# Loading the softmax factors of four attention chunks earlier, and finishing the first chunk on VectorE

## The chip, the cores and the metric

The kernel runs on one core of one Trainium2 chip. Its time is the device time of one execution in microseconds. A core has five engines that run beside each other, each with an instruction queue of its own that is worked off in order: TensorE (PE in the profile; its weight loads are listed as PEld), VectorE (DVE), ScalarE (ACT), GpSimd (POOL) and SyncE (SP). SP, ACT and POOL also issue DMA transfers. An instruction that waits for a semaphore holds up all that stands behind it in its queue.

## The reference, cut to what matters

The input `x` has 2048 rows of 640. Two branches share it. Branch A is attention with 32 heads of 20 over four chunks of 512 rows, softmax within the chunk (where a query's index is below the key's, the logit is pushed down by 1e9), mixed per head with a read from a memory that is summed over the chunks before; its output is multiplied by `wo`. Branch B is a gated feed-forward of width 1728. A gate per row mixes the two.

```
for s in range(4):
    logits = qs @ ks.T * scale + mask
    a_dot  = softmax(logits) @ vs
    a_mem  = (phi(qs) @ M) / (phi(qs) @ z + 1e-6)
    outs.append(g_head * a_mem + (1 - g_head) * a_dot)
    M, z = M + phi(ks).T @ vs, z + phi(ks).sum()
a = concat(outs) @ wo
b = (silu(x @ w1) * (x @ w3)) @ w2
return sigmoid(x . gate_w) * a + (1 - sigmoid(x . gate_w)) * b
```

## The kernel before, in words

All values are 32-bit; most products are made from a high and a low part in three passes (`PASSES`), so that a block of 128 x 512 results takes 15 matmuls over five blocks of 128 inputs. The chunks are handled in pairs, A = (0, 1) and B = (2, 3). For a pair the kernel projects v, k and q, stores q and k to DRAM by heads, and runs feed-forward groups; attention runs beside it all the time.

The order of TensorE's queue is the program's order, written out by hand. It is made by two generators. `attention()` yields 40 slots for each group of four heads; in slot 5 of 40 it emits a large group of score matmuls (`s`, `t`) and the product with v (`o`), in slot 17 a smaller one. In between, `step` takes feed-forward and projection work from a list of jobs, one step at a time; a step of that work is mostly three matmuls and ends with a `yield` of its nominal duration. Each step of it also calls `stores()` (which counts down the stores put off by `store_later`) and `w_step()` (which loads and splits weights ahead of use: two raw buffers, six split ones). The other engines' queues are ordered by Tile's planner: it takes what its own estimates of durations and transfers say is ready, earlier program order first. `here(...)` pins an instruction behind the one traced just before it on its engine. `after(n, f)` calls `f` n slots later; in the tail, a slot is a step.

The softmax denominators are handled at the end. The product with v also sums the probabilities. `pv_quad` stores its result to DRAM (`od`). When a chunk's last heads are done, `o_sums` loads the sums; 22 slots after the last product with v, `o_scale` (L670) turns them into factors `rs` on VectorE and writes them to DRAM, spread over 20 rows a head, in four transfers on ACT's queue (`rd`, L675). `normalize(c)` (L698) then does, for each of five blocks `b` of 128 rows:

- load the factors of the block, `rb`, on ACT's queue (L707), into one of two buffers of the tag `spread`;
- multiply the block of `oall` by it on VectorE (L716);
- for chunks 1 to 3, transpose the memory's part on TensorE into a PSUM bank (L720) and add it on VectorE (L721);
- cast the sum to its high part on ACT (L722) and take the difference as its low part on VectorE (L723).

Loads 0 and 1 are issued in the first step of this generator, load b + 2 at the start of the step after block b. The generator is braided into feed-forward steps: `braid(a, b, every, skip)` takes one step of `b` after each `every` steps of `a`, the first `skip` steps left out. Then `rest` (L783) multiplies by `wo`.

The matmul results go to eight PSUM banks, handed out in rotation. A matmul that begins a bank waits until the engine that empties the bank's last content is through: VectorE for row maxima (L588) and for the copy of an attention result (L638), ACT for exponentials (L620).

`finish(c, fb, ps)` (L508) ends a block of a chunk's output: add the accumulator, multiply by the row gate `shares[c]` (VectorE for odd blocks, POOL for even ones), store on SP's queue; for chunks 0 and 1 the store is put off by two steps. Chunk 0's `finish` lies at the switch from pair A to pair B. The buffer of its accumulator is taken over by pair B's `V`, which POOL first fills with ones (L348); POOL then splits weights (L106) and issues the loads of the k weights (L162).

Of the kernel before, what the change touches and what calls it, by code (L numbers as in the profile page):

```python
# [17 lines left out]
P = 128  # L18
# [20 lines left out]
def gated_mix(ctx: ExitStack, tc: tile.TileContext, xT, wqk, wv, w13, w2, w2h, wo, beta, out):  # L39
# [223 lines left out]
    def store_later(dst, src, key=None, queue=nc.sync, n=4):  # L263
        late.append([n, dst, src, key, queue])
# [177 lines left out]
    def job_read(c):  # L442
        return 5.6, memory_read(c)
# [64 lines left out]
    def finish(c, fb, ps, end=False):  # L508
        dst = accs[c][:, fb]
        for n0 in ((0, 256) if end else (0,)):  # L510
            d, p, g = (t[:, n0:n0 + (256 if end else L)] for t in (dst, ps, shares[c]))
            nc.vector.tensor_add(d, p, d)
            (nc.vector if end or fb % 2 else nc.gpsimd).tensor_mul(d, d, g)
            if c < 2:
                store_later(out[c, fb], d, n=2)
            else:
                nc.sync.dma_start(out[c, fb, :, n0:n0 + d.shape[-1]], d)

    def ffn_down(cs, js, idx, last=()):
        first = js[0] == 0  # L520
# [149 lines left out]
    def o_scale(c):  # L670

        here(nc.vector.reciprocal(rs, rs))
        nc.vector.scalar_tensor_tensor(rs, rs, cR, er, op0=ALU.mult, op1=ALU.mult)
        for a in range(4):
            here(nc.scalar.dma_start(rd[c][:, :, a * P:(a + 1) * P], rs[a::4].unsqueeze(1).broadcast_to([H, DH, P])))  # L675
        turned.append(c)

    shares = {}

    def spread(name):  # L680
        return sp.tile([P, L], F32, tag="spread", name=name, bufs=2)

    def load_share(c):
        shares[c] = spread(f"sh{c}")
# [4 lines left out]
    def load_memory(c):  # L689

        assert ("g", c, 3) in stored
        gms[c] = big_tile(f"gm{c}", FR)[:, :KB * L].rearrange("p (b n) -> p b n", b=KB)
        for qb in range(4):
            here(nc.gpsimd.dma_start(gms[c].bitcast(F32)[:, :, qb * P:(qb + 1) * P],
                                     gd[c][:, qb].rearrange("p (b n) -> p b n", b=KB)))
            yield 1

    def normalize(c):  # L698

        rows = rd[c].rearrange("h e n -> (h e) n")  # L700
        rb = {}

        def load(b):
            if b < KB:
                assert c in turned
                rb[b] = spread(f"rb{c}_{b}")
                here(nc.scalar.dma_start(rb[b], rows[b * P:(b + 1) * P]))  # L707

        load(0)
        load(1)  # L710
        yield 1
        if not c:
            gms[c] = big_tile(f"oT{c}", FR)[:, :KB * L].rearrange("p (b n) -> p b n", b=KB)
        for b in range(KB):
            o, hi = rb[b], gms[c][:, b]
            nc.vector.tensor_mul(o, oall[c][:, b].bitcast(F32), o)  # L716
            if c:
                pt = bank_tile(f"gt{c}_{b}")
                for qb in range(4):
                    nc.tensor.transpose(pt[:, qb * P:(qb + 1) * P], hi[:, qb * P:(qb + 1) * P].bitcast(F32), ident)  # L720
                nc.vector.tensor_add(o, o, pt)  # L721
            nc.scalar.copy(hi, o)  # L722
            nc.vector.tensor_sub(oall[c][:, b], o, hi.bitcast(F32))  # L723
            yield 450 if c else 1
            load(b + 2)

    NJ = NSEG * H

# [81 lines left out]
    def job_up(cs, j):  # L810
        return (4 if j < NF else 2) * 3.5, ffn_up(cs, j, plan_up([j])[0])
# [6 lines left out]
    def job_down(cs, g, last=()):  # L818
        return 2.32 * sum(3 if j < NF else 2 for j in GROUPS[g]), ffn_down(cs, GROUPS[g], plan_down(GROUPS[g]), last)

    def jobs_up(cs, g):
        return [job_up(cs, j) for j in GROUPS[g]]
# [17 lines left out]
    def chain(jobs):  # L840
        return sum(c for c, _ in jobs), (y for _, g in jobs for y in g)

    def braid(a, b, every, skip=0, rest=True):

        def gen():
            n = 0
            for y in a[1]:
                yield y
                n += not isinstance(y, float)
                if n > skip and (n - skip) % every == 0:  # L850
                    z = next(b[1], None)
                    if z is not None:
                        yield z
            if rest:
                yield from b[1]
        return a[0] + b[0], gen()
# [23 lines left out]
    d = job_down(A, 2)  # L880
    u = [job_up(A, j) for j in GROUPS[3][:2]]
    o1, o2 = jobs_oproj(0)
    seg = [d, braid(chain(u), o1, 5), o2] + [job_up(A, j) for j in GROUPS[3][2:]] + [job_down(A, 3)]
    u0, u1 = jobs_up_by_chunk(A, 4)
    x2, x3 = split_x(2), split_x(3)
    seg += [(0, load_raw(2)), (0, load_raw(3))] + u0 + [braid(chain(u1), (0, x2), 4, 0, False)]
# [13 lines left out]
    segs.append((2 * H + LAG + 2, seg))  # L900
    up.append(job_up(B, 2))
    o1, o2 = jobs_oproj(1)
    seg = [braid(chain(up[1:]), o1, 4, 11), braid(o2, job_read(3), 3, 1), job_down(B, 0), braid(chain(jobs_up(B, 1)), (0, load_memory(2)), 5)]
    segs.append((3 * H + LAG + 1, seg))
    d = job_down(B, 1)
    u = [job_up(B, j) for j in GROUPS[2][:2]]
    o1, o2 = jobs_oproj(2)
    seg = [d, braid(chain(u), o1, 5), o2] + [job_up(B, j) for j in GROUPS[2][2:]]
    seg += [job_down(B, 2), braid(chain(jobs_up(B, 3)), (0, load_memory(3)), 5)]
    segs.append((NJ + LAG, seg))  # L910
    d, u = job_down(B, 3), jobs_up(B, 4)
    o1, o2 = jobs_oproj(3)
    tail = [braid(chain([d] + u), o1, 5, 10)] + [o2, job_down(B, 4, B)]

    for n, (_, g) in enumerate(head):
        for _ in g:
# [112 lines left out]
```

## Time and profile before

| | us |
|---|---|
| median of 3 runs (lowest to highest) | 1131.23 (1129.55 to 1133.21) |
| the profiled execution, its own time | 1131.51 |
| its span, first to last instruction | 1129.7 |
| TensorE busy | 1099.9 |
| VectorE busy | 584.8 |
| POOL busy | 494.5 |
| ACT busy | 460.0 |
| mean granted TensorE clock | 0.989 |

The span is one execution; its own time is 1.8 us longer, for what lies around it. A row of the timeline reads: start in us, duration, engine, line, operation, what is written and read, how many merged, and in brackets the idle time of the engine before it with what ended it. A row of a stretch (a:b) reads: its length, the busy time of PE, PEld, DVE, ACT and POOL with instruction counts, the granted TensorE clock as a share of full speed, the busy share of the DMA engines, and GB/s. A row of the waits reads: who waited for whom, in total, how often, the longest. `rd` are the written factors, `rb` a loaded block of them, `gt` the transposed memory part, `oq` the copy of an attention result, `sh` the row gate.

### The profile page before, as it was taken

The page shows a single profiled execution, that of the slowest core. Times are in us where ns is not written, and L with a number is a line of the kernel's source. Part 1 is how long each engine was busy: PE and PEld are TensorE (multiplying, and loading weights), DVE is VectorE, ACT ScalarE, POOL GpSimd, SP SyncE. Part 2 cuts the span into 40 slices and gives each one's busy share as a digit, 9 for nine tenths or more (in the row PEclk, how much of TensorE's full clock was granted, in tenths as well). Part 3 has the DMA queues.
Part 4 walks back from the last instruction along what each step waited for, and adds up shares of the span by engine and source line. Part 5 has one row for each costly group of instructions (what it writes and reads, how often), then busy time and mean ns, then how long its engine had stood idle before and what let it go on. Part 6 is the DMA issues. An engine that isn't in the chain of part 4 may idle for free.

```text
span 1129.7 us, 17927 instructions
## 1 busy us (share of the span) xinstructions
PE 1099.9 (97%) x6265; PEld 856.5 (76%) x6265; DVE 584.8 (52%) x1689; ACT 460.0 (41%) x952; POOL 494.5 (44%) x601
## 2 busy tenths in 40 slices
PE   9999999999999999997999998999999989999998
PEld 6988877777777787785977776676777767777786
DVE  5032564455555455473253675774557665561465
ACT  6165334444243324254255543425544443334140
POOL 4053444354454346353153436444754544454232
PEclk9999999999999999998999999999999999999999
DMA  8265943344354345444286869355655533543323
GB/s 310 97 227 205 268 113 92 89 102 112 84 135 119 107 101 157 127 120 121 98 256 216 290 187 252 106 149 140 169 134 151 142 94 90 118 107 87 112 86 112
DMA packets 99193, 163.29 MB, mean 145 GB/s; under 512 B 10432, under 2 KB 34272, under 8 KB 99104
## 3 DMA queue, kind: packets, MB, share of 16 engines
q1 hardware_dynamic: 61312, 105.91, 29.9%
q0 software_dynamic: 20384, 38.68, 15.6%
q10 hardware_dynamic: 17408, 17.57, 4.9%
q8 instruction: 50, 0.82, 0.3%
q14 instruction: 39, 0.32, 0.1%
HBM read 101.80 MB, written 59.79 MB: 143 GB/s over the span
## 4 chain that ended last, share of the span: by engine, by line
PE 83%; DMA 4%; issue 4%; DVE 3%; POOL 3%; ACT 2%; SPq 0%; ACTq 0%; DVEq 0%; POOLq 0%
PE g L251 16%; PE f L534 15%; PE u L251 15%; PE k L251 6%; PE v L362 6%; PE q L251 6%; PE o L634 5%; PE s L581 4%; PE op L792 4%; PE t L614 3%; DMA rb<-rd 2%; PE pm L425 1%; PE nd L329 1%; POOL W L106 1%; ACT P L620 1%
## 5 line engine op out<-in xcount | busy, mean ns | idle before, releaser
L106 POOL TENSOR_TENSOR W<-wr,W 128x640 fp32r<-128x640 f32 (+1 forms) x126 | 197.0, 1570 | 280.1 <-ACT W L105 255.9
L588 DVE CUSTOM_DVE_ANT_0 junk<-s,mask 128x256 bf16<-128x256 f32 (+3 forms) x512 | 250.0, 488 | 115.3 <-PE s L581 82.9
L620 ACT ACTIVATE P<-t 128x512 f32<-128x512 f32 (+1 forms) x384 | 172.0, 538 | 132.5 <-PE t L614 104.3
L251 PE MATMUL g<-X,W 128*128 128x512 f32 x840 | 211.4, 400 | 2.5 <-DVE m L588 1.4
L251 PE MATMUL u<-X,W 128*128 128x512 f32 x780 | 197.4, 401 | 0.4 <-DVE m L588 0.4
L534 PE MATMUL f<-ht,W 128*128 128x512 f32 x820 | 195.2, 396 | 0.0
L251 PEld LDWEIGHTS g<-X,W 128*128 128x128 f32 x840 | 156.7, 189 | 40.1 <-DVE m L588 2.1
L534 PEld LDWEIGHTS f<-ht,W 128*128 128x128 f32 x820 | 153.1, 188 | 36.7
L624 POOL TENSOR_SCALAR_AFFINE_SELECT P<-P 128x256 f32<-128x256 f32 x192 | 93.4, 497 | 180.7 <-ACT P L620 180.4
L251 PEld LDWEIGHTS u<-X,W 128*128 128x128 f32 x780 | 145.2, 189 | 35.4 <-DVE m L588 0.6
L105 ACT CAST W<-wr 128x640 fp32r<-128x640 f32 (+1 forms) x133 | 95.6, 729 | 152.4 <-DVE acc L542 37.1
L106 POOL TENSOR_TENSOR ht<-ft,ht 128x512 fp32r<-128x512 f32 x52 | 67.8, 1304 | 112.2 <-ACT ht L105 112.2
L558 POOL DMA_DIRECT2D qk<-qkd x128 | 82.9, 649 | 2.3 <-PE t L614 1.2
L581 PE MATMUL s<-qk 60*128 60x256 f32 (+3 forms) x512 | 77.8, 346 | 2.8 <-DVE fu L491 1.0
L634 PE MATMUL o<-P,vg 128*32 128x512 f32 (+3 forms) x1024 | 77.7, 445 | 0.4 <-DVE X L131 0.4
L251 PE MATMUL k<-X,W 128*128 128x512 f32 x300 | 77.0, 403 | 0.7 <-ACT P L620 0.7
L251 PE MATMUL q<-X,W 128*128 128x512 f32 x300 | 75.3, 405 | 1.2 <-ACT X L105 0.4
L614 PE MATMUL t<-qk 62*128 62x256 f32 (+3 forms) x512 | 65.0, 324 | 9.8 <-DVE X L131 5.7
L362 PE MATMUL v<-W,X 128*128 128x320 f32 (+1 forms) x480 | 71.8, 311 | 0.0
L362 PEld LDWEIGHTS v<-W,X 128*128 128x128 f32 x480 | 71.1, 189 | 0.5 <-ACT P L620 0.2
L542 DVE TENSOR_TENSOR acc<-f,acc 128x512 f32<-128x512 f32 x65 | 44.4, 689 | 49.0 <-PE f L534 48.9
L251 PEld LDWEIGHTS q<-X,W 128*128 128x128 f32 x300 | 56.3, 191 | 17.0 <-ACT X L105 1.3
(107 smaller groups left out, 1084.1 us busy)
## 6 DMA issues: line engine op xcount, KB each, us to landing
qk<-qkd POOLq DMA_DIRECT2D x128, 240.0 KB, 4.4
wr<-in_w_dram SPq DMA_DIRECT2D x80, 320.0 KB
qkd<-qs SPq DMA_DIRECT2D x20, 512.0 KB
qkd<-ks SPq DMA_DIRECT2D x20, 512.0 KB
od<-oq SPq DMA_DIRECT2D x32, 256.0 KB
wr<-in_wo_dram SPq DMA_DIRECT2D x20, 320.0 KB
vg<-vd SPq DMA_DIRECT2D x16, 336.0 KB
xr<-in_xT_dram SPq DMA_DIRECT2D x20, 256.0 KB
```

Of the source, the lines that this page charges most:

```text
L105: pin(nc.scalar.copy(dst[:, 0], src))
L106: (lo or nc.gpsimd.tensor_sub)(dst[:, 1], src, dst[:, 0].bitcast(F32))
L251: nc.tensor.matmul(ps, w[:, a, kb * P:(kb + 1) * P], x[:, b, kb, :], start=n == 0, stop=n == 14)
L362: nc.tensor.matmul(ps[:, :n1 - n0], x[:, a, kb, lb * P:(lb + 1) * P], wvt[kb][:, b, n0:n1], start=n == 0, stop=n == 14)
L534: nc.tensor.matmul(ps, w, h, start=n == 0, stop=n == len(ms) - 1)
L558: here(nc.gpsimd.dma_start(t[64 * i:64 * i + RH], qkd[c][RH * (h + i):RH * (h + i + 1)]))
L581: nc.tensor.matmul(ps[i][:, o:o + w], q[:, qb * P:(qb + 1) * P], key[:, :w], start=n == 0, stop=n == len(todo) - 1, skip_group_check=True)
L588: nc.vector.tensor_tensor_reduce(out=junk[:, :w], in0=ps[i][:, o:o + w], in1=mask[:, L - w:], scale=1.0, scalar=-3.0e38, op0=ALU.add, op1= ...
L614: nc.tensor.matmul(ps[i][:, o:o + L - kb * P], key[:, kb * P:(kb + 1) * P], q[:, kb * P:], start=n == 0, stop=n == len(todo) - 1, skip_gro ...
L620: last["exp"] = nc.scalar.activation(pairs[2 * m + k]["P"][:, i, o:o + n], ps[i][:, b:b + n], AF.Exp, scale=SCALE)
L624: nc.gpsimd.affine_select(d, d, pattern=[[0, 2], [0, n], [1, P]], base=0, channel_multiplier=-1, compare_op=ALU.is_ge, fill=0.0)
L634: nc.tensor.matmul(ps[32 * i:32 * i + 32, kb * P:], heads[2 * p + i]["v"][:, kb], pairs[p + i // 2]["P"][:, i % 2, o:o + n], start=kb == 0 ...
```

## The change

Three parts.

1. `o_scale` now hangs the loads of factor blocks 0 and 1 on slots 8 and 9 after the writes (`after(8 + b, load_factor, c, b)`). `normalize` loads them itself only if that hasn't happened.
2. In `normalize`, each block is two steps: one that computes, one that loads block b + 2. The braids take a step every 3 instead of every 5 (every 4 for chunk 1). Block b is computed at step 3 + 6b of the feed-forward work for chunks 0 and 2 (before 10 + 5b), 14 + 6b for chunk 1 (before 19 + 4b) and 13 + 6b for chunk 3 (before 20 + 5b); load b + 2 comes one step of the braid after block b, at 6 + 6b, 17 + 6b and 16 + 6b (before 15 + 5b, 23 + 4b and 25 + 5b).
3. In `finish`, chunk 0 multiplies all five blocks on VectorE, and the stores of chunks 0 and 1 are issued right after the multiplication.

```diff
-            (nc.vector if end or fb % 2 else nc.gpsimd).tensor_mul(d, d, g)
-            if c < 2:
-                store_later(out[c, fb], d, n=2)
-            else:
-                nc.sync.dma_start(out[c, fb, :, n0:n0 + d.shape[-1]], d)
+            (nc.gpsimd if c and fb % 2 == 0 and not end else nc.vector).tensor_mul(d, d, g)
+            nc.sync.dma_start(out[c, fb, :, n0:n0 + d.shape[-1]], d)
...
         turned.append(c)
+        for b in range(2):
+            after(8 + b, load_factor, c, b)
...
+    def load_factor(c, b):
+        if b < KB and (c, b) not in factors:
+            assert c in turned
+            factors[c, b] = spread(f"rb{c}_{b}")
+            here(nc.scalar.dma_start(factors[c, b], rd[c].rearrange("h e n -> (h e) n")[b * P:(b + 1) * P]))
...
     def normalize(c):
-        rows = rd[c].rearrange("h e n -> (h e) n")
-        rb = {}
-        def load(b):
-            if b < KB:
-                assert c in turned
-                rb[b] = spread(f"rb{c}_{b}")
-                here(nc.scalar.dma_start(rb[b], rows[b * P:(b + 1) * P]))
-        load(0)
-        load(1)
-        yield 1
+        load_factor(c, 0)
+        load_factor(c, 1)
...
         for b in range(KB):
-            o, hi = rb[b], gms[c][:, b]
+            o, hi = factors[c, b], gms[c][:, b]
...
             yield 450 if c else 1
-            load(b + 2)
+            load_factor(c, b + 2)
+            yield 1
...
-    seg = [d, braid(chain(u), o1, 5), o2] + [job_up(A, j) for j in GROUPS[3][2:]] + [job_down(A, 3)]
+    seg = [d, braid(chain(u), o1, 3), o2] + [job_up(A, j) for j in GROUPS[3][2:]] + [job_down(A, 3)]
...
-    seg = [braid(chain(up[1:]), o1, 4, 11), braid(o2, job_read(3), 3, 1), job_down(B, 0), braid(chain(jobs_up(B, 1)), (0, load_memory(2)), 5)]
+    seg = [braid(chain(up[1:]), o1, 3, 11), braid(o2, job_read(3), 3, 1), job_down(B, 0), braid(chain(jobs_up(B, 1)), (0, load_memory(2)), 5)]
...
-    seg = [d, braid(chain(u), o1, 5), o2] + [job_up(B, j) for j in GROUPS[2][2:]]
+    seg = [d, braid(chain(u), o1, 3), o2] + [job_up(B, j) for j in GROUPS[2][2:]]
...
-    tail = [braid(chain([d] + u), o1, 5, 10)] + [o2, job_down(B, 4, B)]
+    tail = [braid(chain([d] + u), o1, 3, 10)] + [o2, job_down(B, 4, B)]
```

More of the change, by code (lines that the diff above doesn't have):

```diff
@@ L676, in o_scale @@
         turned.append(c)
-    shares = {}
+        for b in range(2):
+            after(8 + b, load_factor, c, b)
+    shares, factors = {}, {}
     def spread(name):
         return sp.tile([P, L], F32, tag="spread", name=name, bufs=2)
+    def load_factor(c, b):
[3 more added lines that the diff above has]
+            here(nc.scalar.dma_start(factors[c, b], rd[c].rearrange("h e n -> (h e) n")[b * P:(b + 1) * P]))
     def load_share(c):
```

## The prediction

> **What bounds the kernel now.** I read the page first (who is busy), then the same sums in stretches of 15 us (where the busy engine is not), then the timeline of each engine around the bad stretches.
>
> ```profile
> span 1129.7 us, 17927 instructions
> PE 1099.9 (97%) x6265; PEld 856.5 (76%) x6265; DVE 584.8 (52%) x1689; ACT 460.0 (41%) x952; POOL 494.5 (44%) x601
> ...
> 510.00:525.00 15.00, 8.91 (x43) 4.79 (x46) 5.39 (x11) 9.12 (x17) 6.65 (x12) 0.72 0.39 118
> 690.00:705.00 15.00, 11.45 (x89) 7.38 (x87) 7.71 (x24) 6.97 (x15) 8.10 (x12) 0.98 0.79 231
> 705.00:720.00 15.00, 13.61 (x56) 10.84 (x56) 9.71 (x30) 4.28 (x9) 3.68 (x3) 0.79 0.28 77
> 900.00:915.00 15.00, 11.14 (x51) 7.99 (x50) 10.04 (x28) 4.77 (x8) 5.76 (x7) 0.92 0.65 178
> ```
>
> TensorE bounds: 1099.9 of 1129.7 us. A change helps only where TensorE idles or runs at a low granted clock (third number from the right). It does both in three places, and the change speaks to all three: the switch to chunks 2 and 3 (510 to 525), and the normalizing of chunk 1 (690 to 720) and of chunk 2 (900 to 915). The switch as one stretch, then TensorE's own rows, with two undisturbed groups for comparison at the end:
>
> ```profile
> 513.00:522.10 9.10, 3.01 (x13) 1.41 (x16) 4.38 (x9) 6.52 (x14) 3.23 (x8) 0.71 0.57 170
> ...
> 522.02 4.49 PE L634 MATMUL o<-P,vg 128*32 128x512 f32 x32 [0.37 <-DVE X L131]
> ...
> 703.60 0.66 PE L720 MATMUL gt<-ident,gm 128*128 128x128 f32 x4 [2.72 <-DVE m L588]
> 706.64 4.21 PE L251 MATMUL g<-X,W 128*128 128x512 f32 x9 [1.39 <-DVE m L588]
> ...
> 906.74 0.44 PE L614 MATMUL t<-qk 62*128 62x384 f32 x2 [1.89 <-DVE m L588]
> 911.67 0.66 PE L720 MATMUL gt<-ident,gm 128*128 128x128 f32 x4 [1.54 <-DVE m L588]
> 912.71 5.29 PE L251 MATMUL u<-X,W 128*128 128x512 f32 x15 [0.38 <-DVE m L588]
> ...
> 869.44 2.36 PE L634 MATMUL o<-P,vg 128*32 128x512 f32 x32
> 886.09 3.66 PE L251 MATMUL u<-X,W 128*128 128x512 f32 x15
> ```
>
> Prices now, idle plus what the low clock adds: switch 9.10-3.01 = 6.1, plus 4.49-2.36 = 2.1, so **8.2 us**. Chunk 1: 2.72+1.39 = 4.1, plus 4.21 where nine of those fifteen matmuls take 2.2, so 2.0: **6.1 us**. Chunk 2: 1.89+1.54+0.38 = 3.8, plus 5.29-3.66 = 1.6: **5.4 us**. All three gone would be 19.7 us: no outcome lies under 1111.5.
>
> What holds TensorE there is a PSUM bank that VectorE has not emptied. Why VectorE is late in chunks 1 and 2:
>
> ```profile
> DVE rb L716 <- DMA rb<-rd: 22.2, 12, 4.0
> 686.21 6.03 ACTq L675 DMA_DIRECT2D rd<-rs  x4
> 697.05 0.32 ACTq L707 DMA_DIRECT2D rb<-rd  x1
> 702.61 0.73 DVE L716 TENSOR_TENSOR rb<-oall,rb 128x512 f32<-128x512 f32 x1 [2.98 <-DMA rb<-rd]
> ...
> 898.06 0.33 ACTq L707 DMA_DIRECT2D rb<-rd  x1
> 904.70 0.69 DVE L716 TENSOR_TENSOR rb<-oall,rb 128x512 f32<-128x512 f32 x1 [3.96 <-DMA rb<-rd]
> ```
>
> VectorE works in queue order, and the product with a factor (L716) stands in that queue before row maxima that were ready. It waits 2.98 and 3.96 us for a load issued 5.6 and 6.6 us earlier; TensorE stops when its banks run out.
>
> **The change, part by part**, against the profiled execution's 1131.51 us (span 1129.7), which is 0.3 above the median of 1131.23.
>
> Part 1, loads 0 and 1 hang on the factor writes, eight and nine slots behind them, instead of standing in the braid's first step. Count and bytes stay; what moves is their place in ACT's queue, past the exponentials of the next attention group. Now they wait there for the writes to land. The nearest row for that is chunk 3, where the present kernel already loads right behind the writes:
>
> ```profile
> 1055.59 3.42 ACTq L675 DMA_DIRECT2D rd<-rs  x4
> 1062.95 0.87 ACTq L707 DMA_DIRECT2D rb<-rd  x2
> 1065.62 0.69 DVE L716 TENSOR_TENSOR rb<-oall,rb 128x512 f32<-128x512 f32 x1 [3.34 <-DMA rb<-rd]
> 1066.23 0.68 DVE L542 TENSOR_TENSOR acc<-f,acc 128x512 f32<-128x512 f32 x1
> 1071.78 0.60 PE L720 MATMUL gt<-ident,gm 128*128 128x128 f32 x4
> ```
>
> From first write to first load 7.4 us, 3.9 after the last write was issued (1059.0); from load to product 2.7. Tile's planner put that product ahead of the accumulation of 1066.23, which so waited too: out of the wait of 3.34 I estimate that it takes writes and load together for 2 to 3 us faster than they are. This is the change's new wait.
>
> Chunk 1, whose next attention group has these rows:
>
> ```profile
> 693.28 2.36 PE L634 MATMUL o<-P,vg 128*32 128x512 f32 x32
> 696.38 0.57 PE L581 MATMUL s<-qk 60*128 60x384 f32 x4
> 693.98 3.28 ACT L620 ACTIVATE P<-t 128x512 f32<-128x512 f32 x6
> ```
>
> Its writes are issued until 692.24, so they land between 693.6 (7.4 after the first) and 696.1 (3.9 after the last); I take 695, as the issue itself was stretched to 6.0 us. First product then 2.7 to 5.6 us later, 697.7 to 700.6; I take 699 instead of 702.6, some 3.6 earlier. But the planner, off by the same 2 to 3 us, puts it about 696, inside this group, ahead of the copy of the group's result (TensorE is through with it at 695.6); the score matmuls of 696.38 need banks that free behind it. A stop of 2 to 3 us at 696 to 699 takes the place of the 4.1 us that end at 703.60 and 706.64; ACT, held behind the load until 695, delays six exponentials that now start at 693.98 by about 1 us, inside the same stop. The following products are on time. Ends: all 6.1 gone, and 3.4 more than now (idle from 693 to 700, seven for 4.1, plus 0.5 of clock, as ACT's and VectorE's delays add up). Taken: **-2.5**, since a stop of 2 to 3 with its low clock (2.0 now) costs 4 of the present 6.1, and there is a fair chance that the copy goes first.
>
> Chunk 2:
>
> ```profile
> 864.23 3.10 ACTq L675 DMA_DIRECT2D rd<-rs  x4
> 869.36 2.06 ACT L620 ACTIVATE P<-t 128x512 f32<-128x512 f32 x4 [8.53 <-DMA rd<-rs]
> 871.87 0.69 DVE L638 COPY oq<-o 128x512 f32<-128x512 f32 x1 [1.08 <-PE o L634]
> ```
>
> Writes land about 871.3 (3.9 after 867.3). If the load stands before the exponentials of 869.36, they start 1.9 late; the product, ready 2.7 later at 874, can hold the copy of 871.87 for 2.2. So a new stop of 0 to 2.2 at 872 to 875, where TensorE has none now.
>
> Part 2, the braid takes a step every three instead of every five (four in chunk 1), with computing and loading in separate steps. Loads 2 to 4 are written nine TensorE steps (6.3 us at 0.7, a fifth of 886.09's group) before use, not five (3.5), and block 0 of chunk 2 comes at step 3, not 10. Load 2 comes at step 6, not 15: nine steps or 6.3 us before 898.06, about 891.8; a lateness of 6.6 us as at 904.70 would be over by 898.4, well before the stop that ends at 906.74. Load 4 may be the next late one: issued about 901, where load 2's 6.6 us was measured, it could hold VectorE up to 2 us. I let the old 5.4 go and charge 2.4 for the two new places: **-3.0**; ends -5.4 and +1.0 (both stops, 4.2, and 2.2 of clock).
>
> Four more steps per chunk also run the planner of weight loads and splits four steps early; its slots (two raw, six split) are full then, so 0, ends -1 and +1. Chunk 1's last block comes at step 38 of 40 instead of 35: 2 steps and 12 projection matmuls, 4.2 us, cover its chain of product, sum, cast and difference (four of about 0.7, L716's row); 0, up to +1. In chunks 0 and 3 no stop stands in TensorE's rows; 0.
>
> Part 3, chunk 0's result: five products on VectorE instead of two, stores issued at once.
>
> ```profile
> 501.47 0.69 DVE L513 TENSOR_TENSOR acc<-acc,sh 128x512 f32<-128x512 f32 x1 [1.21 <-DMA sh<-ed]
> 504.48 0.68 DVE L513 TENSOR_TENSOR acc<-acc,sh 128x512 f32<-128x512 f32 x1
> 501.51 4.81 POOL L513 TENSOR_TENSOR acc<-acc,sh 128x512 f32<-128x512 f32 x3 [0.68 <-DMA sh<-ed]
> 508.81 0.38 POOL L348 MEMSET V<- 128x128 f32 x1 [2.49 <-DMA out_dram<-acc]
> 509.02 3.11 POOL L106 TENSOR_TENSOR W<-wr,W 128x642 fp32r<-128x642 f32 x2
> 512.06 1.17 POOL L162 DMA_DIRECT2D wr<-in_wqk_dram  x2
> 506.78 1.42 ACT L105 CAST W<-wr 128x642 fp32r<-128x642 f32 x2 [5.91 <-PE f L534]
> 516.85 0.72 ACT L105 CAST W<-wr 128x640 fp32r<-128x640 f32 x1 [2.21 <-DMA wr<-in_wqk_dram]
> ```
>
> The chain: last product 506.32, its store, the memset that reuses the buffer, two weight splits on POOL, the next weight's load, ACT's cast that waits 2.21 for it with the casts and copies of X behind, and TensorE behind those. 504.48 is VectorE's sixth instruction from 501.47, so one each 0.60 us; three more put the last product at 504.48+1.80, ending 506.97: 0.6 later than POOL's. Storing at once saves nothing, since SP issues the last store now at the product's end. All behind shifts: **+0.6**. Ends: -1.5, if the splits pass ahead of the memset (ACT's first cast ends 507.5, not 509.0), and +1.8, the three products in front of the X differences. Chunk 1's stores at once: 0, up to +1 if SP stands at a store with a weight load behind it.
>
> Sum: 1131.51 - 2.5 - 3.0 + 0.6 = 1126.6; against the median, **1126.3 us**.
>
> [...]
>
> **Rivals.**
> *The wait moves and grows (slower).* ACT stands behind writes that haven't landed, in the middle of an attention group, and VectorE behind the product. For: 7.4 us from write to load in chunk 3, and 8 slots are about 4 us. Against: ACT was idle or issuing these writes until 692 and 869 anyway. Price at the upper ends: +3.4 and +1.0, so 1135.6. It decides once the new stops cost over 11.5 us in all.
> *Nothing gained.* A product's place in VectorE's queue follows the planner's landing time, not the step it is written in, so loading earlier moves the place with it, and each stop stays as long as the load's lateness. For: chunk 3's product above, 6 us ahead of the transposes (1071.78) it is written with. Against: away from an attention group a late product costs TensorE nothing. Time: 1131.
> *All hidden.* The products land behind the group's copies, both stops go, nothing new: -6.1-5.4 = 1119.7. For: chunk 3 waits 3.34 and TensorE doesn't stop. Against: the groups lie just where the loads now land.
>
> **How the numbers follow.** Forecast 0.38, all hidden 0.16, nothing gained 0.18, slower 0.28. 0.3% is 3.4 us, about what a measurement of this kernel can tell. Faster (under 1127.8): all hidden and most of the forecast, 0.51; same 0.20; slower 0.29. Forecast alone 1122 to 1130; with the others, 1118 to 1137.
>
> **What would show it.** Right: first factor load of chunk 1 issued about 695, its product before 700, TensorE's idle at 701 to 707 and 905 to 913 gone, a shorter one at 696 to 699; last chunk-0 product about 507. Wrong: TensorE idle of over 4 us at 692 to 700 or any at 870 to 876; or a switch that shrinks by more than 2 us, which would mean that POOL and not the store held the weights.

## The result, and the profile after

The changed kernel takes 1131.96 us (median; 1130.04 to 1136.22) beside 1130.95 (1127.92 to 1133.21) of the kernel before: ratio 1.0012, 95% interval 1.0001 to 1.0023. The forecast was 1126.3, faster. The profiled execution took 1133.55 us, the third longest of fourteen, with a span of 1131.7 (before 1131.51 and 1129.7).

The page, and the stretches of the kernel after that answer to those shown of before (columns as there):

```profile
span 1131.7 us, 17920 instructions
PE 1099.8 (97%) x6265; PEld 855.7 (76%) x6265; DVE 588.0 (52%) x1692; ACT 460.3 (41%) x952; POOL 491.1 (43%) x598
...
510.00:525.00 15.00, 11.02 (x64) 6.10 (x64) 6.39 (x12) 8.98 (x17) 5.59 (x12) 0.78 0.37 118
690.00:705.00 15.00, 5.18 (x40) 2.12 (x38) 4.97 (x10) 4.41 (x8) 3.61 (x4) 0.59 0.45 133
705.00:720.00 15.00, 14.92 (x87) 11.63 (x80) 12.41 (x41) 6.85 (x15) 7.35 (x10) 0.96 0.47 108
870.00:885.00 15.00, 12.26 (x72) 8.61 (x72) 7.53 (x22) 4.26 (x10) 3.42 (x6) 0.77 0.47 130
900.00:915.00 15.00, 14.53 (x106) 10.27 (x105) 11.62 (x28) 9.12 (x18) 9.56 (x11) 1.00 0.51 139
513.00:522.10 9.10, 5.12 (x22) 1.83 (x24) 4.53 (x9) 7.10 (x14) 2.99 (x5) 0.80 0.53 185
```

TensorE's busy time is the same, 1099.8 against 1099.9. Its holes have moved: fewer at the switch and at 900, a new one at 870, and one at 690 where TensorE works 5.18 of 15 us at a clock of 0.59. Since the order of the matmuls is nearly the same in both kernels, a stretch can be measured from one matmul to another in both traces; the difference is what the change costs in that stretch, idle time and clock together (us, by the kernel before's times):

| stretch | TensorE idle before | after | stretch longer by |
|---|---|---|---|
| start to 370 | 2.2 | 2.3 | -1.2 |
| 370 to 410, chunk 0 normalized | 0 | 0.7 | +1.4 |
| 500 to 535, switch | 6.1 | 4.0 | -2.1 |
| 683 to 740, chunk 1 normalized | 6.7 | 9.9 | +2.7 |
| 740 to 862 | 1.5 | 2.0 | +0.7 |
| 862 to 922, chunk 2 normalized | 3.9 | 3.2 | +0.2 |
| the rest | 2.5 | 2.9 | +0.2 |

The sum, +1.9, agrees with the 2.0 by which the spans differ. The first row has no edit in it and moves by up to 1.7 us from run to run below, so a single stretch says something from about 2 us on.

**Switch.** Rows of the timeline of VectorE, POOL, ACT and TensorE of the kernel after:

```profile
507.37 0.68 DVE L513 TENSOR_TENSOR acc<-acc,sh 128x512 f32<-128x512 f32 x1
...
507.79 3.25 POOL L106 TENSOR_TENSOR W<-wr,W 128x642 fp32r<-128x642 f32 x2 [6.80 <-ACT W L105]
510.97 0.38 POOL L348 MEMSET V<- 128x128 f32 x1
511.15 1.15 POOL L162 DMA_DIRECT2D wr<-in_wqk_dram  x2
...
516.17 0.73 ACT L105 CAST W<-wr 128x640 fp32r<-128x640 f32 x1
...
518.66 0.79 PE L611 MATMUL t<-qk 62*128 62x384 f32 x3 [1.71 <-DVE X L131]
```

The last product ends at 508.05, 1.7 us later than before, and yet all behind it is earlier: POOL, free of products, has its two splits ahead of the memset that waits for the stores. The load follows at 511.15 (before 512.06), and ACT's cast waits for nothing (before 2.21). ACT's queue has another order too: the cast now stands behind one more copy of an X block, that of 515.14, where before it stood ahead of that copy (517.97 there), and TensorE's stop of 3.93 us before was a wait for that block. TensorE's longest stop there is now 1.71 us.

**Chunk 1.** TensorE, VectorE and ACT of the kernel after:

```profile
688.49 0.60 PE L715 MATMUL gt<-ident,gm 128*128 128x128 f32 x4
...
690.58 0.74 PE L611 MATMUL t<-qk 62*128 62x512 f32 x6 [0.36 <-DMA qk<-mr]
700.77 4.49 PE L631 MATMUL o<-P,vg 128*32 128x512 f32 x32 [9.46 <-DVE rb L716]
...
698.55 1.37 DVE L711 TENSOR_TENSOR rb<-oall,rb 128x512 f32<-128x512 f32 x2 [5.96 <-DMA rb<-rd]
699.84 0.68 DVE L716 TENSOR_TENSOR rb<-rb,gt 128x512 f32<-128x512 f32 x1
...
694.75 0.81 ACTq L686 DMA_DIRECT2D rb<-rd  x2
695.61 2.06 ACT L617 ACTIVATE P<-t 128x512 f32<-128x512 f32 x4 [3.73 <-DMA rd<-rs]
```

Read from below: the load is issued at 694.75 and the product starts at 698.55, both where the prediction had them (695, 699). But what waits is not the copy of the group's result: it is the product with v itself, 9.46 us. The transposes of block 0 had taken a PSUM bank at 688.49, ahead of the group; the sum at 699.84 frees that bank, the sum needs the product, the product the load. The load also stands ahead of the exponentials of 695.61, before which ACT stands idle for 3.73 us.

**Chunk 2.** The same engines in the kernel after:

```profile
877.07 0.79 PE L578 MATMUL s<-qk 60*128 60x384 f32 x3 [2.74 <-DVE oq L635]
...
892.19 0.60 PE L715 MATMUL gt<-ident,gm 128*128 128x128 f32 x4
...
875.72 0.69 DVE L711 TENSOR_TENSOR rb<-oall,rb 128x512 f32<-128x512 f32 x1 [3.48 <-DMA rb<-rd]
876.33 0.68 DVE L635 COPY oq<-o 128x512 f32<-128x512 f32 x1
```

The old stops at 905 to 913 are gone but for 0.47. The new one, 2.74 us, comes from a product that stands ahead of a copy in VectorE's queue at 875.72, although it is written in the same step as the transposes of 892.19, which TensorE reaches some 16 us later.

### The profile page after: what moved, and what is told of

Same layout as the page of the kernel before. It is cut to its first block, busy times and chain, and to the rows that moved or that the text cites. A ratio compares the mean times of both kernels' runs of the same rounds, so it can differ in the third digit from the quotient of the medians.

```text
span 1131.7 us, 17920 instructions
## 1 busy us (share of the span) xinstructions
PE 1099.8 (97%) x6265; PEld 855.7 (76%) x6265; DVE 588.0 (52%) x1692; ACT 460.3 (41%) x952; POOL 491.1 (43%) x598
## 4 chain that ended last, share of the span: by engine, by line
PE 78%; issue 8%; DMA 5%; DVE 4%; POOL 3%; ACT 2%; ACTq 1%; SPq 0%; DVEq 0%; POOLq 0%
PE g L251 15%; PE f L531 15%; PE u L251 14%; PE q L251 6%; PE k L251 6%; PE o L631 5%; PE op L788 4%; PE s L578 4%; PE v L362 3%; PE t L611 3%; PE pm L425 1%; DVE junk L585 1%; POOL W L106 1%; PE nd L329 1%; DMA rb<-rd 1%
## 5 line engine op out<-in xcount | busy, mean ns | idle before, releaser
L531 PE MATMUL f<-ht,W 128*128 128x512 f32 x820 | 198.4, 400 | 0.0
L631 PEld LDWEIGHTS o<-P,vg 128*32 128x32 f32 x1024 | 31.0, 113 | 54.6 <-issue 44.7
```

The lines of the kernel that those rows point to most:

```text
L531: nc.tensor.matmul(ps, w, h, start=n == 0, stop=n == len(ms) - 1)
L631: nc.tensor.matmul(ps[32 * i:32 * i + 32, kb * P:], heads[2 * p + i]["v"][:, kb], pairs[p + i // 2]["P"][:, i % 2, o:o + n], start=kb == 0 ...
```

## The experiments

All runs in one table. The ratio is to the kernel before, on the same chip; the other columns are the profiled execution: how much longer a stretch is than in the kernel before, with TensorE's idle time in brackets (before: 0; 6.1; 6.7; 3.9).

| run | us | ratio, 95% | chunk 0 | switch | chunk 1 | chunk 2 |
|---|---|---|---|---|---|---|
| changed kernel | 1131.96 | 1.0012, 1.0001 to 1.0023 | +1.4 (0.7) | -2.1 (4.0) | +2.7 (9.9) | +0.2 (3.2) |
| p3_alone | 1129.25 | 0.9987, 0.9970 to 1.0003 | 0.0 (0) | -1.1 (4.7) | -0.1 (6.3) | +0.1 (3.9) |
| p3_now | 1132.13 | one execution | 0.0 (0) | +0.2 (6.2) | +0.7 (7.2) | -1.0 (2.3) |
| p12_only | 1135.71 | 1.0042, 1.0025 to 1.0059 | +0.7 (0.2) | -0.7 (6.0) | +2.7 (10.2) | -0.3 (4.2) |
| p23_nohook | 1128.74 | 0.9979, 0.9964 to 0.9995 | +2.2 (1.9) | -3.0 (3.7) | +2.4 (9.9) | -4.3 (1.9) |
| p1_alone | 1143.76 | 1.0123, 1.0100 to 1.0147 | +1.0 (0.6) | -0.9 (5.9) | +8.7 (12.0) | +3.5 (5.5) |
| turn_later | 1131.76 | 1.0016, 0.9999 to 1.0033 | +0.8 (0.2) | -3.0 (3.7) | +4.0 (9.6) | +0.4 (3.4) |
| free_loads | 1126.49 | 0.9975, 0.9955 to 0.9994 | +1.1 (0.8) | -2.2 (4.0) | -3.3 (3.2) | -1.1 (3.2) |
| skip16 | 1138.25 | 1.0076, 1.0051 to 1.0101 | +0.7 (0.2) | -3.2 (3.7) | +9.0 (12.1) | -1.0 (3.5) |
| pin16 | 1125.37 | 0.9954, 0.9939 to 0.9968 | +0.7 (0.5) | -2.1 (4.0) | -0.2 (4.9) | -4.5 (1.5) |
| pin_old | 1123.72 | 0.9949, 0.9929 to 0.9968 | +0.7 (0.5) | -3.2 (3.7) | -1.5 (5.4) | -4.4 (1.4) |
| pin_hook14 | 1123.69 | 0.9942, 0.9926 to 0.9959 | +1.2 (0.9) | -1.4 (5.1) | -3.2 (5.1) | -4.3 (1.4) |
| pin_alone | 1122.36 | 0.9921, 0.9900 to 0.9943 | +1.2 (0.9) | -0.4 (6.2) | -5.7 (3.2) | -4.6 (1.6) |
| pin_p3 | 1119.85 | 0.9898, 0.9880 to 0.9916 | +1.2 (0.9) | -2.4 (4.0) | -3.5 (3.6) | -4.8 (1.4) |
| pin_p3_again | 1118.18 | 0.9893, 0.9878 to 0.9908 | +0.7 (0.5) | -1.6 (4.7) | -5.6 (3.2) | -3.1 (1.6) |
| pin_p3_c | 1121.34 | 0.9920, 0.9908 to 0.9932 | 0.0 (0) | -2.0 (4.0) | -5.7 (3.2) | -4.5 (1.8) |

### Part 3, whole and half

`p3_alone` is the kernel before with both lines of `finish`; `p3_now` keeps the shared products and only stores at once:

```diff
             (nc.vector if end or fb % 2 else nc.gpsimd).tensor_mul(d, d, g)
-            if c < 2:
-                store_later(out[c, fb], d, n=2)
-            else:
-                nc.sync.dma_start(out[c, fb, :, n0:n0 + d.shape[-1]], d)
+            nc.sync.dma_start(out[c, fb, :, n0:n0 + d.shape[-1]], d)
```

> The kernel before with part 3 alone (chunk 0's five products on VectorE, stores at once). Theory A: the 2.1 us that TensorE's idle time shrank by at the switch (6.1 to 4.0 us) are part 3's, because POOL's weight splits stand ahead of the memset; so the same matmul behind the switch (the first projections after 520) comes 2.0 to 3.0 us earlier relative to the start of the switch, nothing else moves, and the ratio is 0.998 (0.9970 to 0.9985). Rival: the switch shrank because the braids put other work around it, or by chance; then it stays at about 6 us idle, or grows by 0.6 as the prediction had it, and the ratio is 1.000 to 1.001.

> The kernel before with half of part 3: stores of chunks 0 and 1 at once, chunk 0's products still shared with POOL. Theory A (the gain at the switch comes from POOL, which without products splits the weights ahead of the memset): nothing changes, TensorE idles 5.9 to 6.3 us at the switch with a stop of 3.5 to 4 us, and the first k weight is loaded at about 512. Rival (the stores set it): a stop of 1.5 to 2.2 us as in the run of part 3, 4 to 4.7 us idle.

POOL and TensorE in `p3_alone`:

```profile
506.01 3.56 POOL L106 TENSOR_TENSOR W<-wr,W 128x642 fp32r<-128x642 f32 x2 [6.80 <-ACT W L105]
510.51 0.38 POOL L348 MEMSET V<- 128x128 f32 x1 [0.94 <-DMA out_dram<-acc]
...
517.90 0.79 PE L611 MATMUL t<-qk 62*128 62x384 f32 x3 [2.10 <-DVE X L131]
```

and in `p3_now`:

```profile
507.16 0.37 POOL L348 MEMSET V<- 128x128 f32 x1 [2.49 <-DMA out_dram<-acc]
507.36 3.11 POOL L106 TENSOR_TENSOR W<-wr,W 128x642 fp32r<-128x642 f32 x2
...
517.97 0.69 PE L611 MATMUL t<-qk 62*128 62x384 f32 x1 [4.02 <-DVE X L131]
```

The stores alone change nothing in this one execution: the memset still waits 2.49 us ahead of the splits, and the stop of 4.02 stays. With the products on VectorE the order on POOL turns over and the long stop halves. An earlier load isn't the reason: it is issued at 511.08 in `p3_alone` and at 510.41 in `p3_now`, and ACT's cast has it at about 515.4 in both. What differs is ACT's order. In `p3_alone` the cast stands behind the copy of one more X block, in `p3_now` ahead of it (the copy follows at 516.60). ACT in `p3_alone`, then in `p3_now`:

```profile
513.75 0.60 ACT L130 COPY xh<-X 128x512 f32<-128x512 f32 x1
515.42 0.73 ACT L105 CAST W<-wr 128x640 fp32r<-128x640 f32 x1 [0.54 <-DMA wr<-in_wqk_dram]
```
```profile
515.49 0.72 ACT L105 CAST W<-wr 128x640 fp32r<-128x640 f32 x1 [2.31 <-DMA wr<-in_wqk_dram]
```

Both orders, POOL's and ACT's, turn with the products; no run changes one without the other. In the profiles the switch is 1.1 to 3.2 us shorter in the runs with part 3, and from 0.9 shorter to 0.2 longer in those without. `p3_alone` itself is at the low end (1.1, where 2 to 3 were expected), and its timed ratio of 0.9987 doesn't exclude 1.

### Parts 1 and 2

`p12_only` has the changed kernel without the lines of `finish`; `p23_nohook` without the hook; `p1_alone` is the kernel before with the hook and the function it calls:

```diff
-        for b in range(2):
-            after(8 + b, load_factor, c, b)
```

> The changed kernel without part 3 (products of chunk 0 shared with POOL and stores put off, as before). Theory A: parts 1 and 2 together are a loss of 4 to 5 us, 2.8 of it in the normalizing of chunk 1 (a stop of 9 to 10 us at about 701), 1.4 in chunk 0, the rest in single stops under 1 us, and chunk 2 is a draw; the switch idles its old 6 us. Ratio 1.0035 (1.003 to 1.005). Rival: the parts don't add up, since a different order at the switch moves everything behind it; then the stop in chunk 1 is of another size and the ratio nearer to 1.001.

> The changed kernel without the early loads (parts 2 and 3). In chunk 1 the first step of the generator, step 14, loads blocks 0 and 1 just ahead of the group, so by theory C the products and the transposes stand ahead of the group as in the changed kernel: the stop of 8 to 10 us in front of the product with v stays, and is as much part 2's doing as part 1's. In chunk 2 the loads come with step 3, behind the group, so the stop of 2.74 us at 877 goes. Ratio 0.999 to 1.002. Rival (part 1 alone makes the stops): idle in 683 to 740 under 6 us and ratio under 0.997.

> The kernel before with part 1 alone (loads of blocks 0 and 1 hung on the writes; braids, steps and chunk 0's end as before). The prediction's step: -2.5 us in chunk 1 and nothing worse than a stop of 2.2 in chunk 2, 1128. Theory C: the planner moves the products of blocks 0 and 1 with their loads, ahead of the copy of the group's result in chunk 1 and in chunk 2 (written 15 us later), so new stops of 5 to 9 us at 693 to 701 and of 2 to 3 us at about 873 to 877 stand against the old ones of 4.1 in chunk 1, and chunk 2 keeps its own of 3.8, since loads 2 to 4 are as before: a loss of 3 to 7 us, ratio 1.003 to 1.006.

Parts 1 and 2 cost 0.42%, as expected (the profiled execution of `p12_only`, 1131.68 us, is near the lowest of its times, so its columns add up to less). Apart they do different things. Without the hook the close braid gives chunk 2 4.3 us, takes 2.2 in chunk 0 and takes 2.4 in chunk 1, the last by the same stop as in the changed kernel. The ratio of 0.9979 lies a little under the 0.999 to 1.002 that I had expected. TensorE in `p23_nohook`:

```profile
700.53 4.38 PE L631 MATMUL o<-P,vg 128*32 128x512 f32 x32 [9.55 <-DVE rb L714]
```

The hook alone is the worst of all, 1.23%. VectorE and TensorE in `p1_alone`:

```profile
698.85 2.17 DVE L715 TENSOR_TENSOR rb<-oall,rb 128x512 f32<-128x512 f32 x2 [6.10 <-DMA rb<-rd]
700.94 0.68 DVE L638 COPY oq<-o 128x512 f32<-128x512 f32 x1
...
696.49 0.50 PE L614 MATMUL t<-qk 62*128 62x256 f32 x3 [2.09 <-ACT P L620]
701.67 0.79 PE L581 MATMUL s<-qk 60*128 60x384 f32 x3 [4.25 <-DVE oq L638]
```

Block 0 is written at the old place, step 19, and its product still stands ahead of the group's copy. This is the stop that the prediction described, at 4.25 and 2.09 instead of 2 to 3 us; another of 3.81 us follows at 726, and more in chunk 2. The loss was larger than the 0.3 to 0.6% that I had expected.

### What holds TensorE in chunk 1

`turn_later` moves the transposes of block 0 alone, `skip16` the whole block, `free_loads` takes away what the load waits for (it scales the result with numbers of x instead of the factors):

```diff
+            if c == 1 and b == 0:
+                yield 1
             if c:
                 pt = bank_tile(f"gt{c}_{b}")
```
```diff
-    seg = [braid(chain(up[1:]), o1, 3, 11), braid(o2, job_read(3), 3, 1), job_down(B, 0), braid(chain(jobs_up(B, 1)), (0, load_memory(2)), 5)]
+    seg = [braid(chain(up[1:]), o1, 3, 16), braid(o2, job_read(3), 3, 1), job_down(B, 0), braid(chain(jobs_up(B, 1)), (0, load_memory(2)), 5)]
```
```diff
-            here(nc.scalar.dma_start(factors[c, b], rd[c].rearrange("h e n -> (h e) n")[b * P:(b + 1) * P]))
+            here(nc.scalar.dma_start(factors[c, b], xT[c, :, b, :]))
```

> The changed kernel, with chunk 1's first block taking one more step of the braid between its product and its transposes, so that the transposes come behind the attention group (behind 693 us) and not ahead of it; the loads and the product stay where they are. Theory A (the four transposes take a PSUM bank ahead of the group and keep it until the late product lets the sum through): the stop of 9.46 us in front of the product with v goes. The product is still late (about 698.5) and the copy of the group's result stands behind it on VectorE, so a smaller stop of 3 to 6 us is left at 696 to 701 in front of score matmuls; the kernel gains 3 to 5 us on the changed one: ratio to the kernel before 0.997 to 0.999. Rival B (TensorE stops because ACT's exponentials or VectorE's queue stand, whoever holds the bank): a stop of 8 to 10 us stays in the same place and the ratio is 1.001.

> The changed kernel, with the factor blocks loaded from the input x, same size and rows, instead of from the factors just written (so the output is scaled by wrong numbers, and this is only for its time). The loads then wait for no write. Theory A (the stops are the time that the writes need to land): products of chunk 1 wait under 1 us, the stops of 9.46 us at 701 and of 2.74 us at 877 both go, nothing over 1 us is left in the normalizing of chunks 1 and 2, and the kernel is 6 to 10 us faster than before: 0.991 to 0.995. Rival (the loads themselves are late, as their own transfers or ACT's queue need 3 to 4 us after the issue): waits of 2 to 4 us of VectorE for the loads stay, and a stop of over 2 us with them; 0.997 to 1.000.

> The changed kernel with chunk 1's blocks written five steps later (the braid leaves out 16 steps and not 11), so that block 0 is computed at step 19, as in the kernel before, behind the attention group. Theory C (the planner gives the product the place in VectorE's queue that its estimate of the load's landing gives it, whatever step it is written in; the load hangs on the hook, so the place stays): the product still waits until about 698.5 ahead of the copy of the group's result, TensorE idles 8 to 10 us between 683 and 740, and nothing is gained on the changed kernel (1132, ratio 1.001). Rival D (the step in which the block is written sets the place): the product comes behind the group's maxima, waits under 1 us, TensorE idles under 5 us there, and the kernel is some 6 us faster than the changed one (1126, ratio 0.996).

With the transposes moved, the 9.46 us in front of the product with v go, so the bank did hold it. In their place stand two stops (TensorE in `turn_later`):

```profile
695.05 0.49 PE L611 MATMUL t<-qk 62*128 62x256 f32 x3 [2.11 <-ACT P L617]
...
699.99 0.79 PE L578 MATMUL s<-qk 60*128 60x384 f32 x3 [4.01 <-DVE oq L635]
```

One for the exponentials behind the load on ACT, one for the copy behind the product on VectorE; the stretch idles 9.6 us as before, and nothing is gained. I had expected 3 to 5 us of gain: the bank was only the first of three holds, all behind the same load. `skip16` tests whether the step in which a block is written sets the product's place. The block is written behind the group, and VectorE's queue is still

```profile
696.65 2.20 DVE L711 TENSOR_TENSOR rb<-oall,rb 128x512 f32<-128x512 f32 x2 [6.14 <-DMA rb<-rd]
698.77 0.68 DVE L635 COPY oq<-o 128x512 f32<-128x512 f32 x1
```

The step doesn't set the product's place. That the load does, through the planner's estimate of its landing, is inferred: the product stayed where the load was. The median went up to 1138.25, above the 1132 expected by theory C and far from the rival's 1126.

`free_loads` takes the time of the writes out of the loads. The big stop goes (idle 3.2 instead of 9.9), but not as I had expected, and the ratio of 0.9975 is the rival's. The product still waits long (VectorE in `free_loads`):

```profile
689.41 0.69 DVE L711 TENSOR_TENSOR rb<-oall,rb 128x512 f32<-128x512 f32 x1 [6.65 <-DMA rb<-in_xT_dram]
```

It now stands further ahead in the queue, and the load's issue stands behind the four writes on ACT. It waits 6.65 us before the group begins, and that costs TensorE next to nothing: a late product matters by what is queued behind it. In chunk 2 a stop of 1.79 us stays, so there the writes were not the whole of it.

### The products pinned

```diff
-            nc.vector.tensor_mul(o, oall[c][:, b].bitcast(F32), o)
+            here(nc.vector.tensor_mul(o, oall[c][:, b].bitcast(F32), o))
```

`here` keeps a product behind what was traced before it on VectorE. `pin16` is `skip16` with this line; `pin_old` has parts 1 and 3 and this line, with the old braids and steps; `pin_p3` is the kernel before with part 3 and this line, without early loads and close braid; `pin_alone` is the kernel before with this line only.

> As the run with 16 steps left out, and the products of all chunks pinned in VectorE's queue behind what was traced before them, so that the planner can't move them ahead. Theory C: the products come when their loads have long landed (waits under 0.5 us), no stop over 1.5 us is left in the normalizing of chunks 1 and 2 (idle under 3 us in 683 to 740, where before has 6.7, and under 2 us in 862 to 922, where before has 3.9), and with the gain of part 3 at the switch the kernel is at 1122 to 1126, ratio 0.993 to 0.996. Rival E (it is ACT, held behind the loads' semaphores ahead of the exponentials, and not VectorE that stops TensorE): the loads stand where they stood, so a stop of 4 us or more with exponentials as releaser stays at 693 to 700; ratio 0.998 to 1.001.

> Part 3, the early loads and pinned products, but the braids of the kernel before (a step every 5 or 4, computing block b and loading b + 2 in the same pace as before). Theory C: blocks 0 and 1 as with the close braid, no stop from them; blocks 2 to 4 are written and loaded as before, and a pinned product that waits 1 to 3 us for its load holds up only what was written behind it. Idle under 4 us in chunk 1 and under 3 in chunk 2; 1123 to 1127, ratio 0.994 to 0.997, and chunk 0 loses nothing (the changed kernel lost 1.4 us there). If the close braid is needed, it is 3 us or more slower than the run with 16 steps left out and pinned products.

> The kernel before with part 3 and the pinned products; loads and braids stay as before (no early loads, no close braid). Theory F (the early loads bring nothing once the products stand behind the group's maxima, and cost ACT a stand in the middle of the group): the stop of 1.9 to 2.3 us with exponentials as releaser at 695 goes, load 0 issued at about 697 has landed by the product at about 705, idle in 683 to 740 is 3 to 4.5 us, in 862 to 922 1.5 to 3, and the kernel is level with or up to 2 us faster than the same with early loads: ratio 0.993 to 0.996. Rival G (loading early is what the pin needs): a pinned product waits 2 to 4 us for its load and what is queued behind it stops TensorE again; idle in chunk 1 of 6 us or more, ratio 0.997 to 1.000.

> The kernel before with nothing but the products pinned. Against the run that has part 3 too it tells what part 3 is worth: 1 to 3 us (theory A), so 0.995 to 0.998 here. If the pin without part 3 is at 0.994 or under, part 3 is worth nothing behind it.

The pin takes `skip16` from 1.0076 to 0.9954, on the same chip: the place in VectorE's queue was the cause. VectorE's wait for factor loads over the whole kernel falls from 27.2 us in the changed kernel and 22.2 before to 3.6 in `pin_p3` (the rows of the waits in the changed kernel, then in `pin_p3`):

```profile
DVE rb L711 <- DMA rb<-rd: 27.2, 13, 6.0
```
```profile
DVE rb L713 <- DMA rb<-rd: 3.6, 6, 1.2
```

In chunk 1, `pin16` and `pin_old` idle 4.9 and 5.4 us, where I had expected under 3 and under 4. In `pin_old` 1.92 us of what is left is rival E's share: the early loads hold ACT. ACT and TensorE there:

```profile
693.68 0.81 ACTq L686 DMA_DIRECT2D rb<-rd  x2
694.53 3.17 ACT L617 ACTIVATE P<-t 128x512 f32<-128x512 f32 x8 [2.87 <-DMA rd<-rs]
...
695.18 0.50 PE L611 MATMUL t<-qk 62*128 62x256 f32 x3 [1.92 <-ACT P L617]
```

and in `pin_p3`, where the load comes with the block's first step:

```profile
695.47 1.09 ACT L617 ACTIVATE P<-t 128x512 f32<-128x512 f32 x2 [1.82 <-PE t L611]
696.08 0.84 ACTq L704 DMA_DIRECT2D rb<-rd  x2
...
704.01 2.70 DVE L713 TENSOR_TENSOR rb<-oall,rb 128x512 f32<-128x512 f32 x1
```

Issued at 696.08, it has landed when the product comes at 704.01, without a wait; no exponential waits for the load, and the stop of 1.92 is not there; 3.6 us of idle time stay in the stretch. So pinning needs neither part 1 nor part 2; the close braid of `pin16` brings nothing on `pin_old` either. `pin_alone` came out below the 0.994 under which I had called part 3 worthless, but that bound rested on too high a time for `pin_p3`. Side by side on one chip part 3 takes 0.9921 to 0.9898; the intervals overlap, and the 2.1 us that separate the two profiles at the switch agree with it.

### Early loads hung later, and chunk 0

```diff
-            after(8 + b, load_factor, c, b)
+            after(14 + b, load_factor, c, b)
```

makes `pin_hook14` out of `pin_old`. `pin_p3_again` repeats `pin_p3` beside it; `pin_p3_c` pins in chunks 1 to 3 alone:

```diff
-            here(nc.vector.tensor_mul(o, oall[c][:, b].bitcast(F32), o))
+            mul = nc.vector.tensor_mul(o, oall[c][:, b].bitcast(F32), o)
+            if c:
+                here(mul)
```

> Part 3, pinned products, old braids, and the early loads hung 14 and 15 slots behind the writes and not 8 and 9. Theory F (early loads cost because ACT stands for the writes to land, ahead of the group's exponentials): the loads now come behind those, the stop of 1.9 us at 695 goes, and the kernel is level with the one without early loads (1119 to 1121, ratio 0.989 to 0.992). Rival (the early loads cost in another way, by holding the buffers or DMA queues): it stays at 1123 to 1125.

> Part 3 and pinned products once more, as the yardstick for the other two: 1119 to 1121, ratio 0.988 to 0.992.

> Part 3, with the products pinned in chunks 1 to 3 alone. If the loss of 1.2 us (0.94 idle) in chunk 0 is the pin's, where the planner's own place cost nothing, it goes: idle 0 in 370 to 410, and the kernel is about 1 us faster than with all pinned: 1118 to 1120, ratio 0.988 to 0.991. Otherwise level.

The first edit did not do what it was for: at slot 14 the loads still stand ahead of the group's exponentials in ACT's queue. The stop stays, 1.88 us, and so does the time, which fits the reason given for `pin_old` but doesn't test it from another side. On this chip the early loads cost 0.5% (0.9942 against 0.9893, intervals apart). `pin_p3_c` has chunk 0's loss gone, 0 idle, as expected, and yet its ratio is the higher one, 0.9920 against 0.9893, with intervals that just touch. The profiles don't say why: they show the fastest of its five executions (1120.40) and the slowest of the five of `pin_p3_again` (1122.40). That stays open.

The best version is the kernel before with part 3 and pinned products: 1119.85 and 1118.18 us in two measurements, ratios 0.9898 (0.9880 to 0.9916) and 0.9893 (0.9878 to 0.9908).

## Why the prediction was wrong, step by step

The prediction added up -2.5, -3.0, +0.6 and 0 for chunk 1, chunk 2, the switch and chunk 0, -4.9 us in all. The same four stretches measured +2.7, +0.2, -2.1 and +1.4, +2.2 in all. Chunk 1 has the largest share of the difference, 5.2 us.

**Where the bound lies.** Right: TensorE's holes at three places, all of which the change reached. The wait named, a product in VectorE's queue ahead of row maxima, was the right one too; taking it out with one pin brought 0.8%.

**Chunk 1, -2.5; it was +2.7, near the upper end of +3.4.** The step that failed is "a stop of 2 to 3 us at 696 to 699 takes the place of the 4.1 us". The load (694.75 for 695) and the product (698.55 for 699) came when forecast. Two things of their effect were missed. The wait was priced from the product's place at about 696, hence 2 to 3 us; the planner put it right behind the first maxima, at 692.5, and VectorE stood 5.96 us. And the close braid writes the transposes at step 14, ahead of the group: they took a bank whose release hung on that product, so that the group's product with v waited, 9.46 us. The prediction gave that step number itself and didn't ask which bank the four transposes take. With the transposes away (`turn_later`), the two holds that it did name make 6.1 us together, not 2 to 3.

**Chunk 2, -3.0; it was +0.2.** The old stops went but for 0.47 us, and VectorE waited only once for a factor load from 880 to 922, 0.41 us. Part 2 by itself gave 4.3 (`p23_nohook`) of the 5.4 that was let go. The step that failed is the price of the new stop, "0 to 2.2" at 872 to 875: it was 2.74, with the product at 875.72 instead of 874, and the granted clock fell to 0.77 over 870 to 885. Without the hook that stop isn't there.

**Switch, +0.6; it was -2.1.** The step "all behind shifts" failed. Its end at -1.5, splits ahead of the memset, is what happened, with 0.9 us on the load. Besides, ACT's cast came behind one more X copy, an order that the prediction took as fixed; `p3_alone` halves the long stop although its load is issued no earlier than in `p3_now`. The last product came later than forecast (508.05, not 506.97) and it didn't matter, and storing at once by itself changes nothing (`p3_now`).

**Chunk 0, 0; it was +1.4.** No stop stood there before; 0.7 us of idle stand there now. In the kernel after:

```profile
383.18 0.50 PE L611 MATMUL t<-qk 62*128 62x512 f32 x2 [0.36 <-DVE fu L491]
...
400.53 1.67 PE L251 MATMUL u<-X,W 128*128 128x512 f32 x6 [0.33 <-DVE m L585]
...
393.62 2.68 DVE L711 TENSOR_TENSOR rb<-oall,rb 128x512 f32<-128x512 f32 x1 [2.74 <-DMA rb<-rd]
```

A cost of nothing had been taken because nothing stopped there, without asking how much slack there was. The second stop follows the product of 393.62, which waits for its load and holds up the row maxima. The first doesn't hang on a product: `fu` waits for ACT, whose cast of 381.11 had waited 4.38 us for a weight load. Of all that, +1.4 is less than what a single stretch can tell, and the cause of this loss was not tested.

**Rivals.** "The wait moves and grows" names what happened in chunks 1 and 2, though not its time of 1135.6. "Nothing gained" names the reason (`skip16`, `p1_alone`), and its time of 1131 is near the 1131.96 measured; that is partly luck, since the changed kernel loses in chunks 0 and 1 what it wins at the switch. The forecast had 0.38 against 0.46 for these two. The measured time lies in the wide range of 1118 to 1137 and outside the forecast's own 1122 to 1130.

**The clock.** A low clock was counted in with the new stops, and that was right: after the stop of 2.74 us the granted clock was 0.77 over 870 to 885, and at the switch, with no stop over 1.71, it was 0.80 over 513.0 to 522.1.

## What to carry to other kernels

Where a scheduler orders an engine's queue by its own estimate of when a load lands, moving the load moves its consumer too: if the estimate is short, loading earlier puts the wait ahead of more urgent work. Look up what stands behind the consumer in that queue, and pin the consumer before touching the load. And ask of every matmul that is moved ahead which bank it takes, and what must land before that bank comes free.

## What the hardware showed that was not expected

**Like stops, unlike clocks.** The stretch 755 to 785 holds two short stops and no edit. In the kernel after, and then in `pin_alone`:

```profile
755.00:785.00 30.00, 28.16 (x168) 21.38 (x167) 16.00 (x61) 12.86 (x27) 15.14 (x17) 1.00 0.66 174
```
```profile
755.00:785.00 30.00, 28.19 (x177) 20.16 (x177) 12.39 (x47) 13.83 (x28) 12.25 (x17) 0.89 0.49 128
```

The same idle time, 1.8 us, at a full clock in one and 0.89 in the other; the stretch 740 to 862 came out 0.7 and 3.2 us longer than before. The longest stop doesn't decide it: it is 1.23 us in the first and 1.49 in the second, but the kernel after kept the full clock behind a stop of 1.39 (1.00 over 956.33 to 960.06), and in `free_loads` the 32 matmuls of the product with v at 691.40 took 4.05 us behind stops of 0.55 and 0.37, where they take 2.36 at the full clock (762.93 in the kernel after). Outside the first and the last 30 us of the kernel, the stretches at half clock last 10.24, 6.83 and 3.41 us before (from 516.74, 704.48 and 912.69) and 6.83, 13.65 and 6.83 us after (from 518.52, 692.60 and 876.92), one to four times 3.41. What sets where they begin and how long they last, no run isolates.

**A product of 0.69 us that takes 2.70.** The row of 704.01 in `pin_p3` has it, and that of 393.62 above. POOL in `pin_p3` at that time:

```profile
703.34 1.56 POOL L106 TENSOR_TENSOR W<-wr,W 128x640 fp32r<-128x640 f32 x1
704.86 1.29 POOL L106 TENSOR_TENSOR ht<-ft,ht 128x512 fp32r<-128x512 f32 x1
```

POOL's two splits end at 706.15, the product at 706.71. The product ends 0.56 us behind the splits. In the kernel after, all ten VectorE instructions on blocks of `rb`, `oall` and `acc` that add, subtract or multiply and took over 1 us end 0.55 or 0.56 us behind a POOL instruction with two inputs. The products' records begin 0.85 us ahead of the split of 704.86 and 0.55 ahead of one at 394.17 (in the kernel after), and both products end behind the split. That a product waits for the split is inferred from these ends; why it would, no run shows.
